# Picking the diagonal blocks of P*V on VectorE, and one output row in 512-column matmuls, in a decode-attention kernel

## Chip, cores, metric

One core of a Trainium2 chip. The metric is the device time of one execution in microseconds (us), lower is better. Of a profiled execution the page gives the span from the first to the last instruction, which is about 2 us shorter than the device time.

## The reference

Two decode problems, A and B, each with one query token, 32 heads of 128 columns and a cache of 16384 keys. A attends to all keys, B to the last 4096. The two output rows of 512 are concatenated.

```python
q = (x @ wq).reshape(B, Sq, Hq, Dh).transpose(0, 2, 1, 3)
scores = jnp.einsum("bhqd,bhkd->bhqk", q, k) * (Dh ** -0.5)   # B: k, v are the last W = 4096 keys
p = softmax(scores)
o = jnp.einsum("bhqk,bhkd->bhqd", p, v)
return o.transpose(0, 2, 1, 3).reshape(B, Sq, Hq * Dh) @ wo
```

Inputs are bf16. The two K and two V caches that are read make 335.5 MB, the four weight matrices 16.8 MB.

## The kernel before

The caches come in 20 loads of 8.4 MB of K and 8.4 MB of V each (16 loads for A with two heads each, 4 for B with eight). A load has four chunks. Per chunk, VectorE multiplies K by q and folds 128 columns to 64, TensorE adds up the rest with 8 identity matmuls, VectorE finishes the sum, and ScalarE takes the exponential. A *unit* is one group of heads (24 units: 16 of A with two heads, 8 of B with four). P*V of a unit takes 64 (A) or 32 (B) matmuls. Each has four neighbouring keys `e` per partition as 512 columns, so only the blocks where the key of P matches the key of V, a "diagonal", are wanted from the accumulator:

```python
def _pv(nc, cx, u):
    ...  # csum: the sums of exponentials, VectorE
    for t in range(T):
        r = 32 * (t % 4)
        cx.o(nc.tensor.matmul(acc[r : r + 4 * R, :], lhsT=ch.p[:, t % (U // 4), :, :],
                              rhs=u.load.vt[:, k : k + 4, :], start=(t < 4), stop=(t >= T - 4)))
    if u is u.load.units[-1]:
        cx.loads.release(u.load.v_tag)            # the V buffer may be loaded again
    u.acc_sb = cx.accs_pool.tile([P, 4 * DH], F32, tag="accs", name="acc_sb")
    cx.o(nc.scalar.copy(u.acc_sb[:, :], acc[:, :]))

def _fin_fold(nc, cx, u):
    ...  # one matmul: the sum of the exponentials into column DH
    for e in range(4):
        cx.o(nc.tensor.matmul(u.f_ps[0:R, 0:DH], lhsT=cx.sel[:, e, 0:R],
                              rhs=u.acc_sb[:, e * DH : (e + 1) * DH], start=False, stop=(e == 3)))

def _fin_row(nc, cx, u): ...  # VectorE: reciprocal; ScalarE: scale into orow
def _fin_col(nc, cx, u): ...  # TensorE: place orow as columns of oc_ps

def _out(nc, cx, st, j0, n):
    ...
    out = [o[r : r + 1, :] for o, r in zip(cx.out_ps, st.out_rows)]   # A: rows 0 and 32, B: 64 and 96
    for j in range(j0, j0 + n):
        for x in range(2):
            cx.o(nc.tensor.matmul(out[x], lhsT=st.oc[:, j : j + 1],
                                  rhs=st.wo_t[:, j, x * w : (x + 1) * w],
                                  start=(j == 0), stop=(j == J - 1)))
    if j0 + n == J:
        ...  # VectorE casts the first half of the row, ScalarE the second; then one transfer out
```

There are two K buffers and one V buffer. A transfer into a buffer is issued when the reductions (K) or P*V (V) that read it are done. The output weights follow the last V: A's in two pieces, B's in pieces of 16, 8, 4, 2 and 2 of 32 rows a partition, so that B's output row can follow the pieces as they land.

The softmax here doesn't subtract the row's maximum and nothing guards it: scores larger than these inputs give would overflow.

Of the kernel before, what the change touches and what calls it, by code (L numbers as in the profile page):

```python
# [8 lines left out]
F32 = mybir.dt.float32  # L9
BF16 = mybir.dt.bfloat16  # L10
P = 128
ACT = mybir.ActivationFunctionType
ALU = mybir.AluOpType
AX = mybir.AxisListType

DH = 128
# [196 lines left out]
def _pv(nc, cx, u):  # L213

    R = u.R
    u.csum = cx.small.tile([P, R], F32, tag=f"csum{u.st.name}", name="csum")
    cx.o(nc.vector.tensor_reduce(
        out=u.csum[:, :], in_=u.cs[:, :, :].rearrange("p i g -> p g i"), axis=AX.X, op=ALU.add,
    ))
    cx.turn = 1 - cx.turn  # L220
    acc = cx.acc[cx.turn]
    T = u.st.keys // 4
    for t in range(T):
        r = 32 * (t % 4)
        ch, k = u.chunks[4 * t // U], u.k0 + 4 * t
        cx.o(nc.tensor.matmul(  # L226
            acc[r : r + 4 * R, :],
            lhsT=ch.p[:, t % (U // 4), :, :],
            rhs=u.load.vt[:, k : k + 4, :],
            start=(t < 4),  # L230
            stop=(t >= T - 4),
        ))
    if u is u.load.units[-1]:
        cx.loads.release(u.load.v_tag)
    u.acc_sb = cx.accs_pool.tile([P, 4 * DH], F32, tag="accs", name="acc_sb")
    cx.o(nc.scalar.copy(u.acc_sb[:, :], acc[:, :]))  # L236


def _fin_fold(nc, cx, u):
    R = u.R  # L240
    u.f_ps = cx.psf_pool.tile([8, DH + 1], F32, tag="f", name="f_ps")
    cx.o(nc.tensor.matmul(
        u.f_ps[0:R, DH : DH + 1], lhsT=u.csum[:, :], rhs=cx.ones_col[:, 0:1],
        start=True, stop=True, skip_group_check=True,
    ))
    for e in range(4):
        cx.o(nc.tensor.matmul(  # L247
            u.f_ps[0:R, 0:DH],
            lhsT=cx.sel[:, e, 0:R],
            rhs=u.acc_sb[:, e * DH : (e + 1) * DH],  # L250
            start=False, stop=(e == 3), skip_group_check=True,
        ))


def _fin_row(nc, cx, u):
    R = u.R
    recip = cx.small.tile([8, 1], F32, tag="recip", name="recip")
    cx.o(nc.vector.reciprocal(recip[0:R, :], u.f_ps[0:R, DH : DH + 1]))  # L258
    u.orow = cx.small.tile([8, DH], BF16, tag="orow", name="orow")
    cx.o(nc.scalar.activation(  # L260
        out=u.orow[0:R, :], in_=u.f_ps[0:R, 0:DH], func=ACT.Copy, scale=recip[0:R, 0:1]
    ))


def _fin_col(nc, cx, u):

    st = u.st
    J = st.wo.shape[0] // P
    n = DH // J
    last = u.i == len(st.units) - 1  # L270
    for r in range(n):
        at = cx.place_at - n * u.h0 - r
        cx.o(nc.tensor.matmul(  # L273
            cx.oc_ps[:, st.oc_at : st.oc_at + J],
            lhsT=cx.place[0 : u.R, at : at + P],
            rhs=u.orow[0 : u.R, r * J : (r + 1) * J],
            start=(cx.oc_first and r == 0), stop=(last and r == n - 1),
            skip_group_check=True,
        ))
    cx.oc_first = False  # L280


def _out(nc, cx, st, j0, n):
    J = st.wo.shape[0] // P
    if j0 == 0:
        st.oc = cx.singles.tile([P, J], BF16, tag=f"oc{st.name}", name=f"oc{st.name}")
        cx.o(nc.vector.tensor_copy(st.oc[:, :], cx.oc_ps[:, st.oc_at : st.oc_at + J]))
    w = st.DN // 2
    out = [o[r : r + 1, :] for o, r in zip(cx.out_ps, st.out_rows)]
    for j in range(j0, j0 + n):  # L290
        for x in range(2):
            cx.o(nc.tensor.matmul(  # L292
                out[x],
                lhsT=st.oc[:, j : j + 1],
                rhs=st.wo_t[:, j, x * w : (x + 1) * w],
                start=(j == 0),
                stop=(j == J - 1),
            ))
    if j0 + n == J:
        row = cx.accs_pool.tile([1, st.DN], BF16, tag="accs", name=f"row{st.name}")  # L300
        cx.o(nc.vector.tensor_copy(row[0:1, 0:w], out[0]))  # L301
        cx.o(nc.scalar.copy(row[0:1, w:], out[1]))
        cx.o(nc.sync.dma_start(out=cx.out[0, 0:1, st.at : st.at + st.DN], in_=row[0:1, :]))


# [1 line left out]
def kernel(  # L307
# [14 lines left out]
    nc = tc.nc  # L322
# [4 lines left out]
    cx = _Ctx()  # L327
# [22 lines left out]
    def problem(name, x, k_cache, v_cache, wq, wo, sk0, W, at):  # L350
        st = _Problem()
        st.name, st.x, st.wq, st.wo, st.at = name, x, wq, wo, at
        st.R, st.keys = (2, KEYS) if name == "A" else (4, KEYS // 2)
        assert st.R * W == P * st.keys
        st.DN = wo.shape[1]
        st.k_view = k_cache[0, :, sk0 : sk0 + W, :]
        st.v_view = v_cache[0, :, sk0 : sk0 + W, :]
        st.oc_at, st.out_rows = (0, (0, 32)) if name == "A" else (64, (64, 96))
        st.p_pool = cx.p_poolA if name == "A" else cx.p_poolB
        n = KEYS // st.keys * st.R  # L360
        st.loads = [_Load(st, i) for i in range(k_cache.shape[1] // n)]
        st.units = [u for x in st.loads for u in x.units]
        return st

    stA = problem("A", A_x, A_k_cache, A_v_cache, A_wq, A_wo, 0, SkA, 0)
    stB = problem("B", B_x, B_k_cache, B_v_cache, B_wq, B_wo, SkB - WB, WB, A_wo.shape[1])

    loads = []
# [19 lines left out]
    for i, p in enumerate(pieces):  # L388
# [13 lines left out]
        out=cx.ident[:, :],  # L402
        in_=ones[:, 0:P],
# [9 lines left out]
    w = cx.place_at + P  # L413
    cx.place = cx.singles.tile([8, 2 * P], BF16, tag="place", name="place")
    nc.gpsimd.affine_select(
        out=cx.place[:, 0:w],
        in_=ones[0:8, 0:w],
# [4 lines left out]
        channel_multiplier=-n_r,  # L422
    )

    cx.sel = cx.singles.tile([P, 4, 8], F32, tag="sel", name="sel")
    nc.vector.tensor_reduce(
        out=cx.sel[:, :, :].rearrange("p e g -> p g e"),
        in_=cx.ident[:, :].rearrange("p (t g e) -> p g e t", t=4, g=8),
        axis=AX.X,
        op=ALU.add,  # L430
    )
    for st in (stA, stB):
        st.off = cx.singles.tile([P, st.R], F32, tag=f"off{st.name}", name=f"off{st.name}")
        nc.vector.tensor_reduce(
            out=st.off[:, :],
            in_=cx.ident[:, :].rearrange("p (i g) -> p g i", g=st.R),
            axis=AX.X,
            op=ALU.add,
        )
        nc.vector.tensor_scalar(  # L440
            out=st.off[:, :], in0=st.off[:, :], scalar1=-1.0, scalar2=1000.0,
            op0=ALU.add, op1=ALU.mult,
# [3 lines left out]
    for i in range(2):  # L446
# [2 lines left out]
    cx.oc_ps = cx.pst_pool.tile([P, 512], F32, tag="ocp", name="oc_ps")  # L449
    cx.oc_first = True  # L450
    cx.out_ps = [
        cx.psout_pool.tile([P, A_wo.shape[1] // 2], F32, tag=f"out{i}", name=f"out{i}")
        for i in range(2)
    ]

# [6 lines left out]

    def fin_pe():
        for u in fins:
            if u.stage == 0:
                _fin_fold(nc, cx, u)
                u.stage = 1
            elif u.stage == 2:
                _fin_col(nc, cx, u)
                u.stage = 9  # L470
        fins[:] = [u for u in fins if u.stage != 9]

    def fin_dve():
        for u in fins:
            if u.stage == 1:
                _fin_row(nc, cx, u)
                u.stage = 2

    def pv(load):
        for u in load.units:  # L480
            fin_pe()
            fin_dve()
            _pv(nc, cx, u)
            u.stage = 0
            fins.append(u)

    prev = None
    for i, x in enumerate(loads):
        for c, ch in enumerate(x.chunks):
            _mult(nc, cx, ch)  # L490
            if prev is not None:
                _softmax(nc, cx, prev)
            fin_pe()
            _add(nc, cx, ch)
            fin_dve()
            _red(nc, cx, ch)
            if i and c == min(i - 1, 2):
                pv(loads[i - 1])
            prev = ch
    _softmax(nc, cx, prev)  # L500
    fin_pe()
    fin_dve()
    pv(loads[-1])
    while fins:
        fin_pe()
        fin_dve()
    for p in pieces:
        _out(nc, cx, *p)
# [30 lines left out]
```

## Time and profile before

Three runs took 826.41 to 826.67 us, median 826.45.

| | before |
|---|---|
| device time, us | 826.45 |
| span of the profiled execution, us | 824.8 |
| moved, MB; mean GB/s | 352.3; 428 |
| busy us: VectorE, TensorE, ScalarE | 583, 400, 99 |

Lines of the page of before. First the busy times (DVE is VectorE, PE TensorE, PEld its weight loads, ACT ScalarE); then the busy tenths of the transfer engines in 40 slices; then the transfer queues by packets, MB and share of 16 engines' span; then the chain of waits.

```profile
span 824.8 us, 5931 instructions
...
PE 400.4 (49%) x2448; PEld 152.1 (18%) x2448; DVE 583.0 (71%) x307; ACT 98.8 (12%) x441; POOL 1.2 (0%) x8
...
DMA  9999999999999999999999999999999999999997
...
q8 instruction: 19, 0.31, 0.2%
q14 instruction: 8, 0.07, 0.0%
...
DMA 57%; DVE 24%; PE 13%; issue 4%; ACT 1%; another core or an unknown queue 1%; SPq 0%; ACTq 0%; DVEq 0%
```

The transfer engines are full in every slice but the last. The chain of waits gives VectorE 24% and TensorE 13%, but the chain names whoever released a wait, and transfers were moving at the same time. In the trace a 64 KB packet takes 2.42 us (median) on one of the 16 engines, which is 27.1 GB/s, or 433 GB/s for 16. At that rate the 352.3 MB need 813 us.

Groups of the same page (line, engine, operation, output<-input, partitions x elements, count | busy us, mean ns | idle before it and what ended that):

```profile
...
L163 DVE TENSOR_TENSOR kt<-kt,qallA 128x8192 bf16<-128x8192 bf16 x64 | 282.7, 4417 | 118.1 <-DMA kt<-in_A_k_cache_dram 118.1
...
L258 DVE RECIPROCAL recip<-f_ps 2x1 f32<-2x1 f32 (+1 forms) x24 | 3.7, 155 | 90.5 <-PE f_ps L247 90.5
...
L236 ACT COPY acc_sb<-acc 128x512 f32<-128x512 f32 x24 | 14.0, 585 | 195.7 <-PE acc L226 195.7
...
L247 PE MATMUL f_ps<-acc_sb,sel 128*2 128x128 f32 (+1 forms) x192 | 24.9, 272 | 16.3 <-ACT acc_sb L236 16.3
```

VectorE waits 118 us for K to land, and 90.5 us at the reciprocals, for P*V, copy and fold. The copies cost ScalarE 14.0 us and the folds TensorE 24.9 us.

The tail, TensorE's timeline of before (start us, length us, what, count, idle before and releaser):

```profile
...
802.10 3.42 PE L226 MATMUL acc<-vt,p_sb 128*16 128x512 bf16 x32 [5.61 <-DMA vt<-in_B_v_cache_dram]
...
806.26 1.04 PE L247 MATMUL f_ps<-acc_sb,sel 128*4 128x128 f32 x8 [0.43 <-ACT acc_sb L236]
...
808.53 5.32 PE L292 MATMUL out<-wo_t,ocA 128*1 128x256 bf16 x64 [0.28 <-DVE ocA L287]
816.76 1.91 PE L292 MATMUL out<-wo_t,ocB 128*1 128x256 bf16 x32 [2.91 <-DMA wo_t<-in_B_wo_dram]
819.23 1.04 PE L292 MATMUL out<-wo_t,ocB 128*1 128x256 bf16 x16 [0.55 <-DMA wo_t<-in_B_wo_dram]
820.47 1.03 PE L292 MATMUL out<-wo_t,ocB 128*1 128x256 bf16 x12 [0.21 <-DMA wo_t<-in_B_wo_dram]
821.75 0.38 PE L292 MATMUL out<-wo_t,ocB 128*1 128x256 bf16 x4 [0.25 <-DMA wo_t<-in_B_wo_dram]
```

The last P*V ends at 805.52. A's output row runs from 808.53 to 813.85. B's row waits 2.91 us for its weights and pauses again for each later piece. So there is room in the tail before B's row, and the last piece of B's weights decides when it ends.

### The profile page before, as it was taken

To read this page: it belongs to the slowest core of one execution; us is meant where nothing else is said; L and a number is where in the kernel's file an instruction comes from. 1 tells how busy PE (TensorE), PEld (TensorE's weight loads), DVE (VectorE), ACT (ScalarE), POOL (GpSimd) and SP (SyncE) were. 2 spreads that over 40 slices of the span, in tenths; PEclk is the share of its full clock that TensorE was granted. 3 is DMA by queue.
4 is the path that set the end of the run, shared out by engine and by line. 5 is a ranking of instruction groups with operands and counts; after the bars stand their busy time and mean duration, and the time that the engine had idled before them with its cause. 6 is when DMAs were issued, how large, how long until landed. Compare 5 with 4: busy or idle time off the path is not lost.

```text
span 824.8 us, 5931 instructions
## 1 busy us (share of the span) xinstructions
PE 400.4 (49%) x2448; PEld 152.1 (18%) x2448; DVE 583.0 (71%) x307; ACT 98.8 (12%) x441; POOL 1.2 (0%) x8
## 2 busy tenths in 40 slices
PE   3435554456255626265436345365616372535566
PEld 1111211122022202021112111122202121212123
DVE  2099895987469867789194959598556878598900
ACT  1000101111111101011111101101101110101120
POOL 0000000000000000000000000000000000000000
PEclk9856867575677668685767576757658575867578
DMA  9999999999999999999999999999999999999997
GB/s 381 432 458 408 454 411 452 416 446 436 416 454 417 449 420 443 429 428 443 415 444 429 433 432 432 436 418 448 423 424 438 445 418 448 417 429 436 427 423 293
DMA packets 8527, 352.71 MB, mean 428 GB/s; under 512 B 1202, under 2 KB 1204, under 8 KB 1588
## 3 DMA queue, kind: packets, MB, share of 16 engines
q1 hardware_dynamic: 8212, 352.33, 99.0%
q8 instruction: 19, 0.31, 0.2%
q14 instruction: 8, 0.07, 0.0%
q10 hardware_dynamic: 288, 0.00, 0.0%
HBM read 352.32 MB, written 0.00 MB: 427 GB/s over the span
## 4 chain that ended last, share of the span: by engine, by line
DMA 57%; DVE 24%; PE 13%; issue 4%; ACT 1%; another core or an unknown queue 1%; SPq 0%; ACTq 0%; DVEq 0%
DMA kt<-in_A_k_cache_dram 43%; DVE kt L163 13%; DVE kt L172 9%; DMA vt<-in_A_v_cache_dram 7%; PE red L182 6%; PE acc L226 6%; DMA vt<-in_B_v_cache_dram 4%; DMA wo_t<-in_B_wo_dram 4%; DVE sc L200 2%; PE f_ps L247 1%; ACT acc_sb L236 1%; SPq L112 0%; PE out L292 0%; DVE rowB L301 0%
## 5 line engine op out<-in xcount | busy, mean ns | idle before, releaser
L182 PE MATMUL red<-kt,ident 128*128 128x512 bf16 x640 | 254.5, 569 | 370.6 <-DVE kt L172 370.6
L163 DVE TENSOR_TENSOR kt<-kt,qallA 128x8192 bf16<-128x8192 bf16 x64 | 282.7, 4417 | 118.1 <-DMA kt<-in_A_k_cache_dram 118.1
L172 DVE TENSOR_TENSOR kt<-kt 128x4096 bf16<-128x4096 bf16 x80 | 182.2, 2278 | 0.0
L182 PEld LDWEIGHTS <-ident 128*128 128x128 bf16 x640 | 82.7, 131 | 522.2 <-issue 435.9
L226 PE MATMUL acc<-vt,p_sb 128*8 128x512 bf16 (+1 forms) x1280 | 93.3, 450 | 15.6 <-DMA vt<-in_A_v_cache_dram 10.0
L203 ACT ACTIVATE p_sb<-sc,offA 128x64 bf16<-128x64 f32 x128 | 43.5, 341 | 368.3 <-DVE sc L200 368.3
L163 DVE TENSOR_TENSOR kt<-kt,qallB 128x8192 bf16<-128x8192 bf16 x16 | 70.4, 4402 | 0.0
L258 DVE RECIPROCAL recip<-f_ps 2x1 f32<-2x1 f32 (+1 forms) x24 | 3.7, 155 | 90.5 <-PE f_ps L247 90.5
L200 DVE TENSOR_REDUCE sc<-red 128x64 f32<-128x512 f32 x80 | 54.4, 680 | 1.8 <-PE red L182 1.7
L226 PEld LDWEIGHTS <-p_sb 128*8 128x8 bf16 (+1 forms) x1280 | 34.9, 98 | 77.6 <-issue 57.7
L236 ACT COPY acc_sb<-acc 128x512 f32<-128x512 f32 x24 | 14.0, 585 | 195.7 <-PE acc L226 195.7
L203 ACT ACTIVATE p_sb<-sc,offB 128x64 bf16<-128x64 f32 x64 | 21.5, 337 | 99.9 <-DVE sc L200 99.9
L247 PE MATMUL f_ps<-acc_sb,sel 128*2 128x128 f32 (+1 forms) x192 | 24.9, 272 | 16.3 <-ACT acc_sb L236 16.3
L203 ACT ACTIVATION_READ_ACCUMULATOR p_sb<-sc,offA 128x1 f32 x128 | 24.0, 187 | 0.0
L127 PE MATMUL q_ps<-wq_t,scr 128*128 128x512 bf16 x64 | 15.9, 411 | 14.2 <-DMA wq_t<-in_A_wq_dram 13.2
L247 PEld LDWEIGHTS f_ps<-acc_sb,sel 128*2 128x2 f32 (+1 forms) x192 | 14.4, 85 | 22.1 <-ACT acc_sb L236 18.7
L203 ACT ACTIVATION_READ_ACCUMULATOR p_sb<-sc,offB 128x1 f32 x64 | 12.0, 187 | 0.0
L260 ACT ACTIVATE orow<-f_ps,recip 2x128 bf16<-2x128 f32 (+1 forms) x24 | 8.6, 358 | 20.0 <-DVE recip L258 15.7
L127 PEld LDWEIGHTS <-scr 128*128 128x128 bf16 x64 | 6.6, 104 | 23.0 <-DVE scr L99 8.7
L273 PE MATMUL oc_ps<-orow,place 2*128 2x32 bf16 (+1 forms) x96 | 6.3, 176 | 0.7 <-ACT orow L260 0.7
L99 DVE COPY scr<-xTB 128x128 bf16<-128x128 bf16 x4 | 0.7, 318 | 8.2 <-DMA xTB<-in_B_x_dram 8.2
L273 PEld LDWEIGHTS <-place 2*128 2x128 bf16 (+1 forms) x96 | 4.0, 93 | 12.2 <-issue 12.2
(32 smaller groups left out, 40.1 us busy)
## 6 DMA issues: line engine op xcount, KB each, us to landing
kt<-in_B_k_cache_dram SPq DMA_DIRECT2D x8, 4096.0 KB, 40.0
vt<-in_B_v_cache_dram SPq DMA_DIRECT2D x8, 4096.0 KB, 31.6
wq_t<-in_A_wq_dram SPq DMA_DIRECT2D x1, 4096.0 KB, 12.3
wq_t<-in_B_wq_dram SPq DMA_DIRECT2D x1, 4096.0 KB
wo_t<-in_A_wo_dram SPq DMA_DIRECT2D x2, 2048.0 KB, 22.3
wo_t<-in_B_wo_dram SPq DMA_DIRECT2D x1, 2048.0 KB, 26.8
wo_t<-in_B_wo_dram SPq DMA_DIRECT2D x1, 1024.0 KB, 28.8
wo_t<-in_B_wo_dram SPq DMA_DIRECT2D x1, 512.0 KB, 29.5
```

What stands on the lines that cost most here:

```text
L127: cx.o(nc.tensor.matmul(q_ps[:, :], lhsT=st.xb[:, c, g, :], rhs=w[:, g, j * (512 // DH) : (j + 1) * (512 // DH), :], start=(g == 0 and c = ...
L163: cx.o(nc.vector.tensor_tensor(out=k, in0=k, in1=q.rearrange("p (o d) -> p o d", o=1).broadcast_to([P, U, DH]), op=ALU.mult,))
L172: cx.o(nc.vector.tensor_tensor(out=k[:, :, 0 : DH // 2], in0=k[:, :, 0 : DH // 2], in1=k[:, :, DH // 2 : DH], op=ALU.add,))
L182: cx.o(nc.tensor.matmul(ch.red[:, :, :], lhsT=cx.ident[:, :], rhs=ch.unit.load.kt[:, ch.k0 : ch.k0 + U, b * W : (b + 1) * W], start=(b == ...
L200: cx.o(nc.vector.tensor_reduce(out=sc[:, :], in_=ch.red[:, :, :], axis=AX.X, op=ALU.add))
L203: cx.o(nc.scalar.activation(out=ch.p[:, :, g, :], in_=sc[:, :].rearrange("p (t e) -> p t e", e=4), func=ACT.Exp, scale=SCALE, bias=u.st.of ...
L226: cx.o(nc.tensor.matmul(acc[r : r + 4 * R, :], lhsT=ch.p[:, t % (U // 4), :, :], rhs=u.load.vt[:, k : k + 4, :], start=(t < 4), stop=(t >= ...
L236: cx.o(nc.scalar.copy(u.acc_sb[:, :], acc[:, :]))
L247: cx.o(nc.tensor.matmul(u.f_ps[0:R, 0:DH], lhsT=cx.sel[:, e, 0:R], rhs=u.acc_sb[:, e * DH : (e + 1) * DH], start=False, stop=(e == 3), ski ...
L258: cx.o(nc.vector.reciprocal(recip[0:R, :], u.f_ps[0:R, DH : DH + 1]))
L260: cx.o(nc.scalar.activation(out=u.orow[0:R, :], in_=u.f_ps[0:R, 0:DH], func=ACT.Copy, scale=recip[0:R, 0:1]))
L273: cx.o(nc.tensor.matmul(cx.oc_ps[:, st.oc_at : st.oc_at + J], lhsT=cx.place[0 : u.R, at : at + P], rhs=u.orow[0 : u.R, r * J : (r + 1) * J ...
```

## The change

Its intent is to spare ScalarE the copy and TensorE three of four fold matmuls. VectorE multiplies each of the four 128-column blocks of the accumulator, straight from PSUM, by a mask that keeps the matching rows, and adds them up; one matmul then folds the rows. That diagonal becomes a stage of its own, so fold, reciprocal and column come later in the program. A's output row becomes 32 matmuls of 512 columns to one PSUM row, in place of 64 of 256 columns to rows 0 and 32.

```diff
@@ _pv
-    u.acc_sb = cx.accs_pool.tile([P, 4 * DH], F32, tag="accs", name="acc_sb")
-    cx.o(nc.scalar.copy(u.acc_sb[:, :], acc[:, :]))
+    u.acc = acc
+
+def _fin_diag(nc, cx, u):
+    u.ds = cx.small.tile([P, DH], F32, tag="ds", name="ds")
+    cx.o(nc.vector.tensor_scalar(
+        out=u.ds[:, :], in0=u.acc[:, 0:DH], scalar1=cx.mod4[:, 0:1], scalar2=None, op0=ALU.mult))
+    for e in range(1, 4):
+        cx.o(nc.vector.scalar_tensor_tensor(
+            out=u.ds[:, :], in0=u.acc[:, e * DH : (e + 1) * DH], scalar=cx.mod4[:, e : e + 1],
+            in1=u.ds[:, :], op0=ALU.mult, op1=ALU.add))
@@ _fin_fold
-    for e in range(4):
-        ... four matmuls from acc_sb ...
+    cx.o(nc.tensor.matmul(
+        u.f_ps[0:R, 0:DH], lhsT=cx.sel[:, 0:R], rhs=u.ds[:, :], start=False, stop=True, ...))
@@ _out
+    if len(st.out_rows) == 1:                       # A
+        r = st.out_rows[0]
+        out, cols = [cx.out_ps[0][r : r + 1, :]], st.DN
+    else:
+        out, cols = [o[r : r + 1, 0:w] for o, r in zip(cx.out_ps, st.out_rows)], w
...
-        st.oc_at, st.out_rows = (0, (0, 32)) if name == "A" else (64, (64, 96))
+        st.oc_at, st.out_rows = (0, (0,)) if name == "A" else (64, (64, 96))
@@ stages: 0 diagonal (VectorE), 1 fold (TensorE), 2 reciprocal and row, 3 column
```

Cut: the masks (`sel` and `mod4`), the wider PSUM tiles of the output rows, the casts of A's row.

## The prediction

> **What bounds the kernel now.** The input transfers. The page's DMA row reads 9 in 39 of 40 slices; 352.3 MB moved at a mean 428 GB/s. In the trace a 64 KB packet takes 2.42 us on one of 16 engines, 433 GB/s for all (estimate), so the bytes need about 813 us of the 824.8 us span, and 16 packets are in flight from 1.7 us to about 815 us without a gap. The Trainium skill, "DMA: Bandwidth & Descriptors", "Where 436 GB/s comes from", gives a ceiling of 435 GB/s; the trace agrees. VectorE is busy 583 us (71%), TensorE 400, ScalarE 99. The chain of waits names VectorE and TensorE for a third of the span, but transfers queue meanwhile: a K load lands 44 us (median, least 27) after issue, of which some 19 us are its own packets (8.4 MB, estimate). No buffer comes free late enough to starve the queues; only the last 10 us can change.
>
> **The change, costed (groups by form).**
> - Removed: 24 ScalarE copies (585 ns, 14.0 us) and three of four fold matmuls per unit: a unit's fold takes 1.04 us, a quarter remains, 24 x 0.8 = 19 us of TensorE.
> - Added: 96 VectorE operations on 128x128 f32 from PSUM. The reduce of 128x512 f32 from PSUM takes 680 ns; at one element per cycle, 128 columns are about 0.28 us, 1.1 us a unit (estimate), 27 us in all. VectorE becomes about 610 us busy.
> - Moved: VectorE waits for P*V itself instead of copy and fold (about 1.7 us less a unit); fold and reciprocal come a chunk later.
>
> All of this lies beside the transfers: worth 0 us until the last V has landed.
>
> **The tail (timeline before).** Last P*V ends 805.5; A's output row takes 808.53 to 813.85 (64 matmuls of 256); B's row starts 816.76, when its weights land, and follows its pieces until the last lands at 821.75; then matmul, cast, output.
> Afterwards the last-but-one unit's fold is issued behind the last P*V, and the last unit's diagonal behind that one's reciprocal: I expect A's row to start about 0.5 us later, near 809.1. Before, two 256-column matmuls to output rows 0 and 32 ran side by side (0.12 us per pair in B's row); now 32 matmuls of 512 go to one row. "TensorE: Matmul & The Clock Gate", "Back-to-back issue gap", gives 216 ns at full clock and 427 at half; here concurrent groups of 512 columns step 0.427 us at granted clock 0.5, which agrees. With 2 to 3.4 us at half clock, A's row takes 8 to 8.6 us instead of 5.3 and ends near 817.3. Cast and B's column copy add 0.6 us, so B's row starts about 817.9, a microsecond late. Its matmuls need 3.8 us and wait for pieces at 819.23, 820.47 and 821.75, so it catches up before the last; slack is some 0.3 us.
>
> **Prediction: 826.6 us, 825.8 to 827.5 (8 in 10).** Faster by over 2%: 1%. Within 2%: 98%. Slower by over 2%: 1%.
>
> **Right or wrong would show as:** DMA row still 9 in 39 slices; ScalarE about 85 us, VectorE near 610; four operations of 0.25 to 0.3 us per unit; fold group a quarter; A's row 32 matmuls in 8 to 9 us; B's last piece still the releaser of its last matmuls.
>
> **What would make it wrong:** VectorE's extra work delaying a buffer until the queues run dry; a bad clock phase stretching A's row beyond 818 us, adding up to 1 us; the second output row waiting for the first row's transfer, which shares a buffer and is now issued about 3 us later.

## The result

The changed kernel took 826.84 us (median of 6 runs, 826.73 to 827.63) against 826.67 (6 runs, 826.41 to 826.83). The ratio is 1.0005, with a 95% interval of 0.9992 to 1.0017: the same. Ratios here and below are the mean time of one kernel's fast runs over that of the other's of the same rounds, so not quite the ratio of the medians quoted.

The page after, the lines that answer to those of before:

```profile
span 824.8 us, 5627 instructions
...
PE 381.9 (46%) x2272; PEld 135.2 (16%) x2272; DVE 614.5 (75%) x404; ACT 86.4 (10%) x417; POOL 1.2 (0%) x8
...
DMA  9999999999999999999999999999999999999997
...
q8 instruction: 17, 0.28, 0.1%
...
DMA 51%; DVE 30%; PE 10%; issue 7%; another core or an unknown queue 1%; SPq 0%; DVEq 0%
```

TensorE lost 18.5 us of busy time and ScalarE 12.4; VectorE gained 31.5. The transfer row did not change. VectorE's share of the chain of waits rose from 24% to 30%, and the time did not.

Groups of the page after:

```profile
...
L163 DVE TENSOR_TENSOR kt<-kt,qallA 128x8192 bf16<-128x8192 bf16 x64 | 282.2, 4409 | 121.0 <-DMA kt<-in_A_k_cache_dram 121.0
...
L241 DVE TENSOR_SCALAR ds<-acc,mod 128x128 f32<-128x128 f32 x24 | 8.3, 344 | 44.8 <-PE acc L226 44.8
...
L245 DVE SCALAR_TENSOR_TENSOR ds<-acc,mod,ds 128x128 f32<-128x128 f32 x72 | 25.2, 350 | 2.6
...
L258 PE MATMUL f_ps<-ds,sel 128*2 128x128 f32 (+1 forms) x48 | 9.7, 286 | 0.6 <-DVE ds L245 0.6
L305 PE MATMUL out<-wo_t,ocA 128*1 128x512 bf16 x32 | 8.8, 442 | 0.3 <-DVE ocA L296 0.3
```

The diagonal costs 8.3 + 25.2 = 33.5 us. In return VectorE now waits 44.8 us for P*V at the diagonal, where it had waited 90.5 us at the reciprocal. Its wait for K (121.0 us) is as long as before (118.1).

The tail after, TensorE's timeline:

```profile
...
801.13 3.59 PE L226 MATMUL acc<-vt,p_sb 128*16 128x512 bf16 x32 [6.29 <-DMA vt<-in_B_v_cache_dram]
...
808.51 8.75 PE L305 MATMUL out<-wo_t,ocA 128*1 128x512 bf16 x32 [0.28 <-DVE ocA L296]
818.16 3.96 PE L305 MATMUL out<-wo_t,ocB 128*1 128x256 bf16 x64 [0.90 <-ACT rowA L315]
```

A's row now takes 8.75 us instead of 5.32 and ends at 817.26. B's row no longer waits for its first piece: it starts at 818.16, released by ScalarE's cast of A's row, and runs without a pause to 822.12. Before, it ended at 822.13. So the tail of this execution has two chains that end together: the last weights piece, and the output rows.

How fast A's row was computed shows in windows of the changed kernel (window, its length, busy us and count of each engine, mean granted clock of TensorE, transfer share, GB/s):

```profile
...
808.50:811.00 2.50, 2.49 (x8) 0.79 (x9) 0.00 (x0) 0.00 (x0) 0.00 (x0) 0.61 1.03 439
811.00:814.00 3.00, 3.00 (x12) 1.05 (x11) 0.00 (x0) 0.00 (x0) 0.00 (x0) 0.76 0.96 404
814.00:817.30 3.30, 3.26 (x16) 1.09 (x13) 0.00 (x0) 0.00 (x0) 0.00 (x0) 1.00 0.93 377
```

A window counts matmuls only roughly; the starts of the single matmuls in the trace are exact: 0.427 us apart in the slow stretch and 0.216 us apart at full clock, from 812.6 us on. The Trainium skill, "TensorE: Matmul & The Clock Gate", section "Back-to-back issue gap", has 216 ns at full clock, and its formula for the slow clock gives 427 ns for 512 columns; both agree. Before, two 256-column matmuls to different rows went side by side: in the trace before, the pairs of A's row start 0.213 us apart in the slow stretch and 0.110 us apart at full clock, half of the wide matmul's step. The skill's "TensorEngine Tiling (Array Packing)", section "Key Properties", says that different tiles can run matmuls in parallel, and this trace shows it. The wider matmul does not halve the work of the row: it gives up that pairing.

### The profile page after: what moved, and what is told of

Its sections match the earlier page's. It is cut to its first block, busy times and chain, and to the rows that moved or that the text cites. A ratio compares the mean times of both kernels' runs of the same rounds, so it can differ in the third digit from the quotient of the medians.

```text
span 824.8 us, 5627 instructions
## 1 busy us (share of the span) xinstructions
PE 381.9 (46%) x2272; PEld 135.2 (16%) x2272; DVE 614.5 (75%) x404; ACT 86.4 (10%) x417; POOL 1.2 (0%) x8
## 4 chain that ended last, share of the span: by engine, by line
DMA 51%; DVE 30%; PE 10%; issue 7%; another core or an unknown queue 1%; SPq 0%; DVEq 0%
DMA kt<-in_A_k_cache_dram 43%; DVE kt L163 15%; DVE kt L172 11%; PE red L182 6%; DMA vt<-in_B_v_cache_dram 5%; PE acc L226 4%; DMA wo_t<-in_B_wo_dram 4%; DVE sc L200 3%; DVE ds L245 1%; DVE ds L241 0%; DVE recip L267 0%; SPq L112 0%; DVE csum L217 0%; PE f_ps L254 0%
## 5 line engine op out<-in xcount | busy, mean ns | idle before, releaser
L163 DVE TENSOR_TENSOR kt<-kt,qallA 128x8192 bf16<-128x8192 bf16 x64 | 282.2, 4409 | 121.0 <-DMA kt<-in_A_k_cache_dram 121.0
L226 PE MATMUL acc<-vt,p_sb 128*8 128x512 bf16 (+1 forms) x1280 | 86.9, 432 | 18.7 <-DMA vt<-in_A_v_cache_dram 12.4
L226 PEld LDWEIGHTS <-p_sb 128*8 128x8 bf16 (+1 forms) x1280 | 32.5, 95 | 77.8 <-issue 52.5
L241 DVE TENSOR_SCALAR ds<-acc,mod 128x128 f32<-128x128 f32 x24 | 8.3, 344 | 44.8 <-PE acc L226 44.8
L245 DVE SCALAR_TENSOR_TENSOR ds<-acc,mod,ds 128x128 f32<-128x128 f32 x72 | 25.2, 350 | 2.6
L217 DVE TENSOR_REDUCE csum<-cs 128x2 f32<-128x8 f32 (+1 forms) x24 | 3.5, 145 | 9.3 <-PE f_ps L254 9.3
L258 PE MATMUL f_ps<-ds,sel 128*2 128x128 f32 (+1 forms) x48 | 9.7, 286 | 0.6 <-DVE ds L245 0.6
L305 PE MATMUL out<-wo_t,ocA 128*1 128x512 bf16 x32 | 8.8, 442 | 0.3 <-DVE ocA L296 0.3
## 6 DMA issues: line engine op xcount, KB each, us to landing
wq_t<-in_A_wq_dram SPq DMA_DIRECT2D x1, 4096.0 KB, 12.4
wo_t<-in_B_wo_dram SPq DMA_DIRECT2D x1, 512.0 KB, 31.5
```

The lines of the kernel that those rows point to most:

```text
L163: cx.o(nc.vector.tensor_tensor(out=k, in0=k, in1=q.rearrange("p (o d) -> p o d", o=1).broadcast_to([P, U, DH]), op=ALU.mult,))
L245: cx.o(nc.vector.scalar_tensor_tensor(out=u.ds[:, :], in0=u.acc[:, e * DH : (e + 1) * DH], scalar=cx.mod4[:, e : e + 1], in1=u.ds[:, :], o ...
L258: cx.o(nc.tensor.matmul(u.f_ps[0:R, 0:DH], lhsT=cx.sel[:, 0:R], rhs=u.ds[:, :], start=False, stop=True, skip_group_check=True,))
L305: cx.o(nc.tensor.matmul(out[x], lhsT=st.oc[:, j : j + 1], rhs=st.wo_t[:, j, x * cols : (x + 1) * cols], start=(j == 0), stop=(j == J - 1),))
```

## The experiments

Theory T: the transfers carry the kernel, everything but the last 10 us lies beside them, and in the tail the row of A has used up what room there was. Rival R: the equal time is a balance, VectorE's added work costs and the other parts give back.

**E1 and E2: each part alone.** E1 is the changed kernel with A's row as before; E2 is the kernel before with the new row of A.

```diff
# E1, against the changed kernel
-        st.oc_at, st.out_rows = (0, (0,)) if name == "A" else (64, (64, 96))
+        st.oc_at, st.out_rows = (0, (0, 32)) if name == "A" else (64, (64, 96))
# E2, against the kernel before: _out and the line above as in the changed kernel, nothing else
```

> The diagonal and the single fold matmul alone; A's output row in two halves as before. Theory (transfers carry the kernel, VectorE's extra work lies beside them): 826.5 to 826.9 us, VectorE about 614 us busy, A's row again 64 matmuls in 5 to 5.5 us, B's last matmuls released by the last weights piece. Rival (the two parts cancel: VectorE, a third of the chain of waits, costs, and the wider row gives back): at least 3 us slower than before.

> A's row as 32 matmuls of 512 columns to one row alone; the copy on ScalarE and four fold matmuls as before. Theory: 826.5 to 827.0 us, A's row 8 to 9 us, B's row starts near 818 and just catches up with the last piece. Rival (parts cancel): at least 2 us faster than before.

E1: 826.42 us (5 runs, 826.34 to 827.07) against 826.53 of before on the same chip; ratio 1.0000 (0.9988 to 1.0013). VectorE was busy 614.5 us. A's row took 5.39 us again, and B's row waited for its weights:

```profile
...
808.70 5.39 PE L305 MATMUL out<-wo_t,ocA 128*1 128x256 bf16 x64 [0.28 <-DVE ocA L296]
816.50 5.42 PE L305 MATMUL out<-wo_t,ocB 128*1 128x256 bf16 x64 [2.42 <-DMA wo_t<-in_B_wo_dram]
```

E2: median 826.49, ratio 1.0005 (0.9993 to 1.0018), but its five runs fall in two groups: 826.33, 826.49 and 826.49, then 827.44 and 828.08. The profiled run was that of 827.44:

```profile
...
806.37 1.87 PE L247 MATMUL f_ps<-acc_sb,sel 128*4 128x128 f32 x8 [0.40 <-ACT acc_sb L236]
...
809.49 8.91 PE L296 MATMUL out<-wo_t,ocA 128*1 128x512 bf16 x32 [0.28 <-DVE ocA L287]
819.37 3.66 PE L296 MATMUL out<-wo_t,ocB 128*1 128x256 bf16 x64 [0.96 <-ACT rowA L306]
```

Here the old fold took 1.87 us instead of 1.04, at a granted clock of 0.50 from 805.5 to 808.5 us where the profiled run of before had 1.00; A's row began 0.96 us later than before, and B's row ended at 823.03, 0.9 us later. R falls: neither part moves the time by the microseconds that a balance would need. What shows in E2 is the used-up room: when the last steps run at a low clock, the end moves. (Only this run of the five was profiled; that the run of 828.08 was alike is not shown.)

**E3 and E4: how much room the tail has.** Each matmul of A's row is done twice, in the changed kernel (E3) and in the kernel before (E4). A's output is doubled. Their outputs are wrong, which doesn't matter for the times.

```diff
-    for j in range(j0, j0 + n):
+    reps = 2 if st.name == "A" else 1
+    for j, rep in [(j, r) for j in range(j0, j0 + n) for r in range(reps)]:
...
-                start=(j == 0), stop=(j == J - 1),
+                start=(j == 0 and rep == 0), stop=(j == J - 1 and rep == reps - 1),
```

> The changed kernel with each matmul of A's row done twice (A's output comes out doubled, wrong on purpose). Theory (the changed kernel has used up the slack of the tail: B's row runs from 818.2 to 822.1 us without a pause): the 32 extra matmuls of 0.216 us push the end by their full 6.9 us, to 833 to 834.5 us. Rival (the end is set by the last weights piece with slack left): under 829 us.

> The kernel before with each matmul of A's row done twice (A's output doubled, wrong on purpose). Theory (before, B's row waited 2.9 us for its weights and then paused for each piece): the 32 extra pairs of 0.11 to 0.12 us, some 3.6 us, are swallowed but for at most 0.7 us: 826.4 to 827.2 us. Rival (the output rows were on the chain already): 829.5 to 830.5 us.

E3: 833.66 us (4 runs, 832.63 to 834.17), ratio to before 1.0082 (1.0067 to 1.0098). That is 6.8 us over the changed kernel's 826.84 (of other rounds), the full length of the added matmuls. Its profiled run:

```profile
...
808.79 16.16 PE L306 MATMUL out<-wo_t,ocA 128*1 128x512 bf16 x64 [0.28 <-DVE ocA L296]
825.84 3.66 PE L306 MATMUL out<-wo_t,ocB 128*1 128x256 bf16 x64 [0.90 <-ACT rowA L316]
```

E4: 827.59 us (4 runs, 827.19 to 828.26), ratio 1.0013 (1.0000 to 1.0027), 1.1 us over before. The median of E4 lies 0.4 us above the range that I had given. Its timeline:

```profile
...
809.50 9.19 PE L293 MATMUL out<-wo_t,ocA 128*1 128x256 bf16 x128 [0.28 <-DVE ocA L287]
819.36 3.66 PE L293 MATMUL out<-wo_t,ocB 128*1 128x256 bf16 x64 [0.67 <-DVE ocB L287]
```

The doubled row took 9.19 us, 3.87 us more than before, and the time rose by 1.1: the tail of before swallowed the larger part. It may have swallowed all of it: in this profiled run A's row already began 0.97 us late (809.50 against 808.53), because the fold before it, which the edit does not touch, ran at a granted clock of 0.50 as in E2, and the run ended only 0.9 us later than before. Whether the other three runs of E4 were alike is not known. The changed kernel has no such room left. The "slack of some 0.3 us" of the prediction was none.

**E5 and E6: what the change is worth where transfers do not bind.** V is loaded once and used for all loads (wrong), so that 193 MB are moved. E5 is that edit of the kernel before, E6 of the changed kernel.

```diff
@@ _load_kv
+    if which == "vt":
+        load.v_tag = tag
+        if cx.v_once is not None:
+            load.vt = cx.v_once
+            return
     t = pool.tile([P, KEYS, DH], BF16, tag=tag, name=which)
+    if which == "vt":
+        cx.v_once = t
```

(The last V, which went to a K buffer, is taken from the same tile.)

> The kernel before with V loaded once and used for all loads (wrong on purpose): 193 MB to move instead of 352, some 446 us at the measured rate, so computation binds. Estimate: first K at 42 us, 80 chunks of 7.14 us, some 3.9 us of wait for P*V, copy and fold in each of 24 units, then the weights: 720 to 750 us. To be compared with the same edit of the changed kernel.

> The changed kernel with V loaded once and used for all loads (wrong on purpose), to be compared with the same edit of the kernel before. Theory (VectorE's four operations of 0.35 us per unit are paid for by not waiting for copy and fold, some 1.7 us): 0 to 12 us faster than the kernel before with V once. Rival (where transfers do not hide it, VectorE's added 33 us show): 15 to 35 us slower than that kernel.

E5: 710.50 us (4 runs, 709.68 to 713.97), below the estimate of 720 to 750 (which had some 94 us of waits for P*V, copy and fold; the trace has 62.7, below). E6: 711.31 us (4 runs, 707.46 to 712.41). The two were run in different rounds and on different chips, and their runs overlap. Against the kernel before in the same rounds the ratios are 0.8604 (0.8586 to 0.8622) and 0.8591 (0.8566 to 0.8615). I call the difference unclear. The loss of 15 us or more that the rival expected is not there; of the 0 to 12 us of gain that the theory expected, no more than a few microseconds can be. The waits say why. Lines of the view of waits (engine and line, what it waited for, us in total, times, longest), first E5, then E6:

```profile
...
DVE recip L264 <- PE f_ps L253: 62.7, 21, 7.2
```

```profile
...
DVE ds L247 <- PE acc L232: 31.9, 20, 6.0
```

E5 has VectorE busy 581.5 us and waiting 62.7 at the reciprocals, 644.2 together; E6 has it busy 613.6 us and waiting 31.9 at the diagonals, 645.5 together. The added work fills time that VectorE used to spend waiting. So even where computation binds, the diagonal neither gains nor loses more than a few microseconds.

**E10: VectorE's added work once more.** The changed kernel with the diagonal done twice (same result).

```diff
+    for _ in range(2):
+        _diag(nc, cx, u)          # the four operations
```

> The changed kernel with the four diagonal operations done twice (same result): VectorE some 33 us busier again, about 648 us. Theory (VectorE's work lies beside the transfers, with more than 33 and less than 96 us of room): 826.6 to 827.8 us, a small part of a microsecond of it from the last unit's second diagonal in the tail. Rival (the added VectorE time is already at its limit): over 829 us.

828.33 us (5 runs, 828.25 to 829.29) against 826.62, ratio 1.0025 (1.0011 to 1.0038): 0.5 us above my range. VectorE was busy 647.6 us. In the body nothing changed: counted from the trace's packets, the 16 engines had less than 0.01 us of empty time between 5 and 815 us, as in the kernel before, and the last piece of weights landed at 821.5 us against 821.3. All of it is in the tail:

```profile
...
808.59 0.59 PE L263 MATMUL f_ps<-ds,sel 128*4 128x128 f32 x2 [2.17 <-DVE ds L250]
...
810.43 8.67 PE L310 MATMUL out<-wo_t,ocA 128*1 128x512 bf16 x32 [0.28 <-DVE ocA L301]
820.00 3.66 PE L310 MATMUL out<-wo_t,ocB 128*1 128x256 bf16 x64 [0.90 <-ACT rowA L320]
```

The second diagonal of the last unit delays A's row from 808.51 to 810.43, and B's row from 818.16 to 820.00. The end follows: B's row ends at 823.66 instead of 822.12, again without room. I had counted a small part of a microsecond for that.

**E9: a version meant to win, by fewer TensorE instructions.** E1 with a second folding addition (64 columns to 32), so that a chunk needs 4 identity matmuls instead of 8. The result is correct.

```diff
@@ _add
+    cx.o(nc.vector.tensor_tensor(
+        out=k[:, :, 0 : DH // 4], in0=k[:, :, 0 : DH // 4], in1=k[:, :, DH // 4 : DH // 2], op=ALU.add))
@@ _red
-    nb = DH // 2 // W
+    nb = DH // 4 // W
```

> A correct kernel made to win: the diagonal-only kernel with a second folding addition on VectorE (64 columns to 32, 80 more operations of about 1.2 us, VectorE about 710 us busy), so that each chunk needs 4 reduction matmuls instead of 8: 640 TensorE instructions less, 2 to 3 fetches fewer. Theory (transfers bind with VectorE having some 120 us of waits for K to give away, and fetches on rings decide the end): 824.8 to 826.0 us. Rival (VectorE is near enough to the bound that 96 us more show): over 828 us.

830.25 us (5 runs, 829.08 to 831.55), ratio 1.0046 (1.0034 to 1.0059): slower by half a per cent, clear of noise. The rival held here. The page's busy times and the wait for K:

```profile
...
PE 274.8 (33%) x1984; PEld 94.8 (11%) x1984; DVE 710.9 (86%) x484; ACT 86.5 (10%) x417; POOL 1.2 (0%) x8
```

```profile
...
DVE kt L163 <- DMA kt<-in_A_k_cache_dram: 51.1, 10, 17.6
```

VectorE at 711 us has used up 70 of the 121.0 us that it waited for K in the changed kernel, and K buffers come free later. The third K transfer is issued at 77.89 us instead of 74.34 (the changed kernel), that of the sixth load at 180.94 instead of 171.82. From the packets, some of the transfer engines stood empty four times, at 80, 177, 296 and 490 us (at the worst, near 179 us, three of 16 still moved), worth 2.3 us of all 16. That is more than half of the 3.8 us by which the last weights landed later than in E1; the packets of the caches and weights also took 2.0 us more per engine in sum (818.8 against 816.8 us), for a reason that I have not found. So the theory that VectorE lies beside the transfers holds for the 32 and the 65 us of added work of E1 and E10, and not for the 128 us of E9. It is not the amount alone that differs: the second fold stands in every chunk between the landing of K and the release of its buffer, and the diagonal does not. With the diagonal done twice (E10) the third K transfer was still issued at 74.46 us. No run separates amount from place.

**E7 and E8: instruction fetches.** The prediction had no account of why the last piece lands at 821.3 us when the bytes at 433 GB/s would be there by about 815 (813 us after the first transfer at 1.7). The page lists 19 packets of instructions on q8, each 16 KB, and in the trace each takes 1.07 us (median). A packet does not name its engine, but each transfer leaves 16 completion marks, one for each engine, and an engine that falls behind stays behind. From those marks and packets of the trace before, worked out:

```
K or V transfer      q8 fetches    first to last mark   marks over 2.5 us
begins landing, us   so far        us                   behind the first
 60.8                 0            0.31                  0
157.6                 2            1.67                  0
351.2                 7            1.79                  0
448.1                 9            3.35                  1
641.7                14            3.37                  6
738.5                16            3.37                  9
787.0                17            4.93                 10
```

The spread grows by 1.4 to 1.6 us at the first, the ninth and the seventeenth fetch, as if the fetches went round 8 of the 16 engines; six engines never fall behind by more than 0.8 us. The engine with the most fetches then lands the last piece. That is not the whole distance from 815 us: the marks of the last piece come at 819.2 us on average and at 821.7 last, so uneven engines cost 2.5 us. The rest is mostly that packets smaller than 64 KB move fewer bytes a second: the packets of the data queue q1 add up to 99.0% of the span of 16 engines, 816.6 us and not 813. (The expectations call an engine's queue a ring.) To test the fetches, E7 adds instructions to E1 (weight loads nobody uses, where TensorE idles), and E8 takes instructions away (half of P*V, wrong).

```diff
# E7
+    if ch.unit.load.chunks.index(ch) < 2:
+        for _ in range(56):
+            cx.o(nc.tensor.ldweights(cx.ident[:, 0:1]))
# E8
-    for t in range(T):
+    for t in range(T // 2):
```

> The diagonal-only kernel plus 2,688 weight loads of one column on TensorE whose weights nobody uses, placed where TensorE idles (after the reductions of the first two chunks of each load): about 10 more 16 KB instruction fetches. Theory (each fetch holds one of the 16 transfer rings for over a microsecond, and the ring with the most fetches lands the last weights piece: in the trace of before the spread between the first and the last ring grew from 0.3 us at 60 us to 4.9 us at 787 us, in steps at the fetches): one more round of fetches over the rings, 827.5 to 829.5 us. Rival (fetches are hidden, the spread has another source): 826.3 to 826.9 us.

> The diagonal-only kernel with the second half of each unit's P*V matmuls left out (wrong on purpose): 640 matmuls and 640 weight loads less, about 5 fetches fewer. Theory (fetches on rings): the fullest ring has one fetch less, 824.6 to 825.5 us. Rival: 826.3 to 826.9 us.

E7 as built adds 2,240 weight loads (56 in two chunks of each of 20 loads), not the 2,688 that I wrote down, and its page has 26 fetches where E1's has 18: eight more, not ten. E7: 828.56 us (5 runs, 828.13 to 829.09) against 826.62, ratio 1.0023 (1.0009 to 1.0037), as expected. Fetch lines of the pages of E7 and E8:

```profile
...
q8 instruction: 26, 0.43, 0.2%
```

```profile
...
q8 instruction: 13, 0.21, 0.1%
```

In E7 the 25th fetch, at 787 us, took the spread from 5.1 to 6.6 us, and the last piece landed at 823.0 us instead of 821.0 in E1. B's row followed it:

```profile
...
811.14 5.33 PE L308 MATMUL out<-wo_t,ocA 128*1 128x256 bf16 x64 [0.28 <-DVE ocA L299]
...
823.50 0.38 PE L308 MATMUL out<-wo_t,ocB 128*1 128x256 bf16 x4 [0.26 <-DMA wo_t<-in_B_wo_dram]
```

A's row was done at 816.5, so it is not what delayed the end. Nor did a buffer come free late: between 5 and 815 us the 16 engines had 0.01 us of empty time. E8: 825.88 us (5 runs, 825.56 to 826.21), ratio 0.9992 (0.9979 to 1.0004). The interval holds 1, though all five runs lie below all nine of before (826.22 to 826.86). The gain is 0.7 us, not the 1.1 to 2 that I had expected. Its last piece landed at 820.5; the spread stood at 3.4 us until 738 us and went to 4.0 at 758, where the trace has one of the 8 KB fetches of q14. I take it that the engine that serves q14 is then the last one, but no run separates that. So: instruction fetches do decide which engine lands last, at the size of a microsecond or two; E7 shows it, E8 leans the same way.

**E11 and E12: moving bytes to other engines.** If 8 engines carry the fetches, others could carry more of the weights. The Trainium skill, "DMA: Bandwidth & Descriptors", section "Why a DMA increments its semaphore by 16 and not by 1", says that a transfer takes the largest number of engines, at most 16, that divides its slowest dimension, and the lowest-numbered of them. By that rule one of 8 partitions would use the lowest 8; no run here shows which ones these did use. So one piece of B's weights went out as 16 transfers of 8 partitions, in E1's kernel.

```diff
+    step = 8 if st.name == "B" and n == J // 8 else P        # E12: n == J // 4
+    for p0 in range(0, P, step):
+        ... dma_start of partitions p0 to p0 + step
```

> Made to win by moving bytes between rings: the diagonal-only kernel with one piece of B's output weights (4 of 32 rows a partition, 0.5 MB) sent as 16 transfers of 8 partitions each[...]. Theory (half of the rings end some 3 us late for their instruction fetches, and these 8 rings are mostly among the others): last weights piece about 1 us earlier, 825.2 to 826.2 us. If the 8 rings are the ones with the fetches: 827.3 to 828.5 us. Rival (rings are not what the end waits for): 826.3 to 826.9 us.

> The same with the piece of 8 rows a partition (1 MB), twice the shift[...]. Theory: 824.3 to 826.6 us, no better than the smaller shift where one of the 8 rings was late already. If the 8 rings carry the fetches: 828.5 to 830.5 us. Rival: 826.3 to 826.9 us.

E11: 831.51 us (5 runs), ratio 1.0060 (1.0047 to 1.0072). E12: 834.72 us (4 runs), ratio 1.0097 (1.0083 to 1.0111). Neither expectation fits, because the edit brought another wait. SyncE's timeline of E11, the issues of the weights pieces and of the output rows:

```profile
...
788.15 35.66 SPq L145 DMA_DIRECT2D wo_t<-in_B_wo_dram  x20
823.91 0.27 SPq L320 DMA_DIRECT2D out_dram<-rowA  x1
```

The 20 issues of B's weights took 35.7 us, where the 5 of before took 2.71; the last pieces and A's output row were issued only at about 823 us. Each issue took 0.27 to 0.43 us, and SyncE stood between them, up to 9.5 us, for nothing that the profile names. So the times of these two runs say nothing on the engines. The marks say a little: each small transfer left one mark when it was issued and eight as its data landed, so it did run on eight engines. The first one's eight came at 814.8, 814.9, 814.9, 815.8, 817.6, 818.2, 818.5 and 820.1 us; the whole piece before it landed from 814.5 to 819.9. So four of the eight were among the engines that lag, the last one included, and neither supposition held. Which engines by number carry the fetches stays open.

No correct version that I ran beats the kernel before by more than noise. E1 equals it.

## Why the prediction was right

- *The transfers bind; the change lies beside them.* Right. 433 GB/s by packets against the 435 GB/s that the skill's "DMA: Bandwidth & Descriptors", section "Where 436 GB/s comes from", gives as ceiling. The engines stayed full in both kernels, and E10 shows that 33 us more still leave them full. E9 bounds it: with the second fold, at 711 us of VectorE, engines run partly empty. That "only the last 10 us can change" missed one thing: the end of the transfers itself moves with the number of instruction fetches (E7).
- *Removed and added work.* ScalarE 86.4 us (predicted about 85). VectorE 614.5 us (predicted about 610); the term was too small: 0.344 and 0.350 us an operation against my 0.28, 33.5 us against 27. The fold went from 24.9 to 9.7 us, not down to a quarter: 15.2 us saved against 19. The wait that VectorE saves, 90.5 to 44.8 us less 9.3 us of new waits at `csum`, is 36.4 us, 1.5 us a unit against my 1.7.
- *A's row starts 0.5 us later.* In the profiled execution it started at 808.51 against 808.53, because P*V also ended 0.80 us sooner, at 804.72. That was luck: the last V landed sooner, and so the row ended at 817.26, near the 817.3 that I had, though it took longer than I had thought (below): two errors cancelled. P*V of the last unit begins between 801.1 and 801.3 us in the profiled runs of after, E1, E3 and E10, and between 802.0 and 802.1 in those with the old fold (before, E2, E4). The marks of the transfer at 787 us are 3.9 us apart in after and 4.9 in before, whose seventeenth fetch came by then; so the fewer instructions are the likely cause, which I had not foreseen. From the end of P*V to A's row it was 3.79 us against 3.01: 0.78 us more, where I had 0.5. The order of steps was as predicted (VectorE's timeline after):

```profile
...
805.28 0.15 DVE L267 RECIPROCAL recip<-f_ps 4x1 f32<-4x1 f32 x1 [0.24 <-PE f_ps L258]
805.36 0.32 DVE L241 TENSOR_SCALAR ds<-acc,mod 128x128 f32<-128x128 f32 x1
805.72 1.12 DVE L245 SCALAR_TENSOR_TENSOR ds<-acc,mod,ds 128x128 f32<-128x128 f32 x3
```

- *A's row takes 8 to 8.6 us, B's row starts near 817.9.* 8.75 us and 818.16. Part of the difference is a wait that I had not seen: both casts of A's row now read one PSUM tile, and ScalarE's half started only after VectorE's (817.75 against 817.30), where before both started at 813.96 and 813.98; B's first matmul then waited for ScalarE's.
- *B's row catches up, slack 0.3 us.* It ended at 822.12, before at 822.13, but with no slack at all (E3, E10). I had also named as a sign that the last piece would still release the last matmuls; it did not, B's row ran from 818.16 without waiting for any piece. That term was mis-sized, and it is why E2, with the old fold before the wide row, was 0.9 us late in its profiled run.
- *What would make it wrong.* No buffer starved, and the second row's cast did not wait for the first row's transfer: it started at 822.21, before at 822.22.

## What to carry to other kernels

Where all transfer engines were full from end to end, moving work between the compute engines was worth nothing, though it saved TensorE 18.5 us and ScalarE 12.4, and VectorE's growing share of the chain of waits did not tell otherwise; look at whether buffers still come free in time, and at what follows the last transfer. A tail that looks unchanged may have lost its room: doubling one step in it shows that at once. One matmul of 512 columns to one PSUM row was no cheaper here than two of 256 to rows 0 and 32, which ran side by side: 0.216 us against 0.110 at full clock.

## What the Trainium skill lacked or had wrong

- "Runtime: NRT & Kernel Launch", section "Instruction fetch mechanics", calls the cost of a 16 KiB boundary "mostly hidden". Where transfers bind it was not: a 16 KB fetch took 1.07 us of a transfer engine, the spread between engines grew to 4.9 us over 17 fetches, and eight more fetches (E7 against E1) cost 2 us.
- "DMA: Bandwidth & Descriptors", section "Where 436 GB/s comes from", has the memory side, about 358 GB/s a core, bind a load from HBM. Here a program on one core loaded at a mean of 428 GB/s and at 433 by full packets. (A note just above that section limits the 358 to both cores of a pair streaming; the section leaves this out.)
- "VectorE: DVE Perf Modes", the table of the section on the TRN2 errata, gives 120 + FD cycles at 0.96 GHz from PSUM, 258 ns for 128 columns (an estimate from that row). The section warns that the row is too low for one SBUF case and says nothing of PSUM. The masked multiply took 344 ns and the multiply-add 350 ns (means of 24 and 72).
- No page that I read says how long SyncE is held when it issues many small transfers behind large ones: 20 issues took 35.7 us (E11), against 2.71 us for 5. What held it is not shown.
